# Attention sums as one block behind each head's scores, the two products of the third score bank swapped, and the first eight late-modulation rows moved from head 36 to head 49

## The chip, the cores and the metric

The kernel runs on one core of a Trainium2 chip. The metric is the device time of one execution in microseconds (us); lower is better. Before the change three timed executions took 2225.91, 2229.25 and 2231.14 us, a median of 2229.25 us.

## The reference

One transformer-like block on x of 2048 tokens by 1024 channels: a compressive-memory attention and then a token-mixing MLP, both modulated by six rows made from a condition c. Cut to what matters:

```python
mod = (silu(c) @ w_mod).reshape(1, 6, 1, -1)            # sa, ca, ga, sb, cb, gb
h = layernorm(x) * (1 + ca) + sa
# attention: 32 heads of 32 channels, 4 segments of 512 tokens
for s in range(4):
    logits = q[s] @ k[s].T * scale + mask               # causal inside the segment
    a_dot = softmax(logits) @ v[s]
    a_mem = (phi(q[s]) @ M) / (phi(q[s]) @ z + 1e-6)    # memory of earlier segments
    o[s] = g * a_mem + (1 - g) * a_dot
    M, z = M + phi(k[s]).T @ v[s], z + phi(k[s]).sum()
x = x + ga * (concat(o) @ wo)
h = layernorm(x) * (1 + cb) + sb
x = x + gb * mixer(h)                                   # y = W2 gelu(W1 layernorm(h))
```

`sa` and `ca` are needed at the start. The four other rows of the modulation are needed only after the attention: they are the "late" rows here.

## The kernel before

**Tasks and heads.** The attention runs in two passes over the tokens: segments 0 and 1 for all eight groups of four heads, then segments 2 and 3. A task t is one group and one segment, so there are 32 tasks of 4 heads, and the loop counts 128 heads n = 4t + h: heads 0 to 63 are the first pass, 64 to 127 the second. What belongs to head h of task t carries both numbers in its name: `sz_7_0` is task 7, head 0.

**What one head does.** `project` makes a task's k, v and q on TensorE (PE) with 256-column products (`nps`, L192) and 512-column products (`qps`, L200), splits of full precision into two parts. `maxima` makes the logits once to find each query's largest one: four products (L478) fill three PSUM banks in turn, `sx` (128 and 256 columns), `sy` (384) and `sz` (512), out of a pool `s1` of two banks; VectorE (DVE) reduces each bank (L480). So the fill of one bank waits until DVE has read the bank two fills before it. `scores` makes the logits again, transposed and with the maximum folded in: three banks `a0` (L515, 512 columns), `a1` (L518, 384) and `a2` (L521 with 128 columns, then L522 with 256), out of a pool `s2` of two banks; ScalarE (ACT) takes the exponential of each (L516, L519, L523) into `p32`, GpSimd (POOL) sets the masked corners to zero (L526), ACT rounds to fp16 (`ph`, L528) and POOL makes the remainder (L530, held in `p32`).

**The sums.** `values` multiplies these weights by v: 20 short products (L544) into one bank `pv`, ten with the rounded part `ph` (97 columns) and then ten with the remainder (65 columns). DVE then takes a reciprocal (L547), a reduction (L549) and a scaling (L551). `values` of a head is called two heads after its `scores` (VL = 2), `maxima` of a head three heads before (LEADS = 3).

**Order.** The code is written in one order, but the framework's scheduler chooses the order of each engine's instructions from its own timeline, within the dependences and within `tc.issue_after`: each instruction in such a block comes behind the given one on that one's engine. `behind(n, engines)` uses it with the instructions noted in `marks`. On the chip each engine runs its list strictly in order and waits where an operand or a buffer is not ready.

**Late rows.** 32 blocks of w_mod (512 KB each) are loaded by `mod_fetch` into a buffer of the pool `raw` (three buffers, shared with the loads of weights) and reduced on DVE by `mod_late` (L573). `later(n, fetch, m, f, engines)` puts the load at head n and the use at head m. Block j below 8 is loaded at head 36 + 2j and used two heads later; block j from 8 on at head 44 + 2j and used one head later. After block 7, `mod_rows(0, 8)` writes the first row out, and head 62 (`spread(gaw, 0)`) reads it back. Around heads 36 to 50 the weights of the eighth group are split (`split_part`, L119 on ACT and L122 on DVE), and from head 51 on the stored h pages of segments 2 and 3 are loaded (`reload_h`).

After the attention come the output products (L791), the norms, and the mixer (L921), which is the longer half of the run.

Of the kernel before, what the change touches and what calls it, by code (L numbers as in the profile page):

```python
# [18 lines left out]
P = 128  # L19
# [8 lines left out]
NV = 97  # L28
# [3 lines left out]
VL = 2  # L32
ML0 = 36
# [8 lines left out]
def attention_and_mlp(ctx, tc, x, wq, wkv, wo, beta, w1, b1, w2, b2, c, wm_a, wm_b, out):  # L42
    nc = tc.nc
    V, A, G, T, SY = nc.vector, nc.scalar, nc.gpsimd, nc.tensor, nc.sync
# [451 lines left out]
    marks = {}  # L496

    @contextmanager
    def behind(n, engines):

        with ExitStack() as s:
            for e in engines:
                if (n, e) in marks:
                    s.enter_context(tc.issue_after(marks[n, e].ins))
            yield

    def scores(t, h):
        d = st[t]
        n = 4 * t + h
        q, k = d["sk", h][:, 0], d["sk", h][:, 1]  # L510
        p32 = r_.tile([P, 1280], F32, tag="p32", bufs=3, name=f"p32_{t}_{h}")
        hi, lo = r_.tile([P, 1280], F16, tag="ph", bufs=3, name=f"ph{t}_{h}"), p32.bitcast(F16)[:, 0:1280]
        d["ph", h] = hi, lo
        b0 = bank("s2", 2, f"a0_{t}_{h}")
        T.matmul(b0, k[:, 0:128], q, start=True, stop=True)  # L515
        A.activation(p32[:, 0:512], b0, AF.Exp, scale=SCALE, bias=shift)  # L516
        b1_ = bank("s2", 2, f"a1_{t}_{h}")
        T.matmul(b1_[:, 0:384], k[:, 128:256], q[:, 128:512], start=True, stop=True)  # L518
        A.activation(p32[:, 512:896], b1_[:, 0:384], AF.Exp, scale=SCALE, bias=shift)  # L519
        b2_ = bank("s2", 2, f"a2_{t}_{h}")  # L520
        T.matmul(b2_[:, 0:128], k[:, 384:512], q[:, 384:512], start=True, stop=True)  # L521
        T.matmul(b2_[:, 128:384], k[:, 256:384], q[:, 256:512], start=True, stop=True)  # L522
        A.activation(p32[:, 896:1280], b2_[:, 0:384], AF.Exp, scale=SCALE, bias=shift)  # L523
        for base, step in ((0, 512), (896, 128)):
            w = bass.AP(tensor=p32.tensor, offset=p32.offset + base, ap=[p32.ap[0], [step, 2], [1, 128]])
            G.affine_select(w, w, pattern=[[0, 2], [1, 128]], compare_op=ALU.is_ge, fill=0.0, base=0,  # L526
                            channel_multiplier=-1)
        marks[n, "A"] = A.copy(hi, p32)  # L528
        for c in (slice(0, 640), slice(640, 1280)):
            marks[n, "G"] = G.tensor_tensor(lo[:, c], p32[:, c], hi[:, c], op=ALU.subtract)  # L530

    def values(t, h):
        pr, g, seg = its[t]
        d = st[t]
        am, ph = d["am"], d["ph", h]
        pv = bank("pv", 1, f"pv{t}_{h}").rearrange("p (a n) -> p a n", a=4)
        col = {0: lambda i: 128 * i, 1: lambda i: 512 + 128 * (i - 1), 2: lambda i: 1024 + 128 * (i - 2),
               3: lambda i: 896}
        n = 0
        for part, w in ((0, NV), (1, 65)):  # L540
            for i in range(4):
                for j in range(i + 1):
                    o = col[j](i)
                    T.matmul(pv[:, i, 0:w], ph[part][:, o:o + 128], d["vp"][:, j, h, 0:w], start=(n == 0),  # L544
                             stop=(n == 19), skip_group_check=True)
                    n += 1
        V.reciprocal(pv[:, :, 0], pv[:, :, 0])  # L547
        red = r_.tile([P, 4, 32], F32, tag="red", bufs=2, name=f"red{t}_{h}")
        V.tensor_reduce(red, pv[:, :, 1:97].rearrange("p a (c e) -> p a e c", c=3), axis=AX.X, op=ALU.add)  # L549
        ah = am[:, :, 32 * h:32 * h + 32]  # L550
        V.scalar_tensor_tensor(red if seg else ah, red, gate[:, 1, 4 * g + h:4 * g + h + 1],  # L551
                               pv[:, :, 0:1].to_broadcast([P, 4, 32]), op0=ALU.mult, op1=ALU.mult)
        if seg:
            G.tensor_tensor(ah, ah, red, op=ALU.add)
        if h < 3:
            return
        ps = bank("ms", 1, f"ops{t}")
        for i in range(4):
            T.transpose(ps[:, 128 * i:128 * i + 128], am[:, i], ident)
        ot = r_.tile([P, L], F32, tag="ot", bufs=1, name=f"ot{t}")  # L560
        A.copy(ot, ps)
        SY.dma_start(oT[g, :, L * seg:L * seg + L], ot)
        del st[t]
# [3 lines left out]
    def mod_fetch(j):  # L567
        r = a.tile([P, D], F32, tag="raw", bufs=3, name=f"rawm{j}")
        SY.dma_start(r, wm_b[P * j:P * j + P])
        return r  # L570

    def mod_late(j, r):
        V.scalar_tensor_tensor(r, r, 1.0, scb, op0=ALU.mult, op1=ALU.mult, accum_out=mcol[:, j:j + 1])  # L573
        if j == 7:
            mod_rows(0, 8)
        if j == 31:
            V.tensor_scalar_add(mcol[:, 16:24], mcol[:, 16:24], 1.0)
            mod_rows(8, 32)
# [14 lines left out]
    def at(f, n):  # L593
        if 0 <= n < 4 * NI:
            f(n // 4, n % 4)
# [62 lines left out]
    def later(n, fetch, m, f, engines):  # L658

        got = []  # L660
        plan(n, lambda: got.append(fetch()))
        plan(m, lambda: f(got[0]), engines)
# [8 lines left out]
    for g in range(2, NG):  # L671
        n = 8 * g - 13
# [3 lines left out]
                  n + n1, lambda r, g=g, kind=kind, part=part: split_part(g, kind, part, r), "A")  # L676
        plan(n + 4, lambda g=g: keep_w(g))
    for j in range(32):
        n = ML0 + 2 * j + (8 if j >= 8 else 0)
        later(n, lambda j=j: mod_fetch(j), n + (2 if j < 8 else 1), lambda r, j=j: mod_late(j, r), "V")  # L680
    plan(WO0 - 3, lambda: spread(gaw, 0))
    for i in range(8):
        n = WO0 + WOS * i
        later(n, lambda i=i: wo_fetch(i), n + 1, lambda r, i=i: wo_split(i, r), "G")

    for n in range(-LEADS, 4 * NI + VL):
        at(scores, n)
        at(maxima, n + LEADS)
        at(values, n - VL)
        m = n + LEADP  # L690
        if 0 <= m + 4 < 4 * NI:
            t = (m + 4) // 4
            if its[t][:2] not in W:
                with tc.issue_after(last_sk[t - 2 if t > 16 else 0, 3].ins):
                    load_w(its[t][1], its[t][0])
        if m >= 8:
            at(project, m)
        if 59 <= m < 67:
            seg, ct = 2 + (m - 59) // 4, 2 * ((m - 59) % 4)
            with ExitStack() as s:  # L700
                if seg == 3:
                    s.enter_context(tc.issue_after((last_sk[15, 3] if ct < 4 else last_nt[14, 3]).ins))
                reload_h(seg, ct)
                reload_h(seg, ct + 1)
        if 4 * NI - 5 <= m < 4 * NI + 3:
            i = m - 4 * NI + 5
            for c in (2 * (i % 4), 2 * (i % 4) + 1):
                wop[c, i // 4] = new_page(f"wo{c}_{i // 4}")
                if c < 5 or i < 4:
                    SY.dma_start(wop[c, i // 4].bitcast(F32), wos[c, i // 4])  # L710
        for f, engines in todo.pop(n, ()):
            with behind(n, engines):
                f()
# [427 lines left out]
```

## Time and profile before

| | before |
|---|---|
| median of three executions | 2229.25 us |
| the profiled execution's own time | 2226.6 us |
| its span, first to last instruction | 2224.9 us |
| PE busy | 2190.3 us, 98% of the span |
| DVE busy | 1666.7 us, 75% |
| ACT, POOL busy | 1135.7 us (51%), 725.8 us (33%) |
| granted TensorE clock, mean | 0.997 |

A busy time counts from the start of an instruction to its end. Matmuls are pipelined, so their records overlap: the distance from one start to the next is what a matmul costs PE, and the length of its record is longer. In a timeline, rows of equal instructions that follow each other are merged; the columns are start, length, engine, line, operation, output and inputs, shape and count, and in brackets the idle time before and what ended it. "PEld" is the weight load that goes with each matmul. "PEclk" is the share of the full TensorE clock that was granted.

### The profile page before, as it was taken

What the parts mean: (1) busy time and instruction counts of PE and PEld (TensorE: products, weight loads), DVE (VectorE), ACT (ScalarE), POOL (GpSimd) and SP (SyncE); (2) the same over time, 40 slices, a digit from 0 to 9 for tenths busy, and PEclk for the clock granted to TensorE, in tenths of its full rate; (3) what the DMA queues carried; (4) which work ended last, traced back from release to release, by engine and by line L of the source; (5) the groups of instructions that cost most, each with busy time, mean ns of one, the idle gap of its engine ahead of it and who ended that gap; (6) DMA issues with size and microseconds to landing.
All of it is one profiled execution on the core that took longest, in us unless ns stands there. A gap on an engine that the chain in (4) does not pass through costs nothing.

```text
span 2224.9 us, 38052 instructions
## 1 busy us (share of the span) xinstructions
PE 2190.3 (98%) x13786; PEld 1881.0 (85%) x13786; DVE 1666.7 (75%) x3762; ACT 1135.7 (51%) x2050; POOL 725.8 (33%) x831
## 2 busy tenths in 40 slices
PE   8999999999999999999999999999999999999999
PEld 5988898888999999888888888888888888888887
DVE  7676777756777777664858766888888886969687
ACT  5486776756666666654636533533334242424232
POOL 2175766646767776663002200033330000000000
PEclk9999999999999999999999999999999999999999
DMA  7666666686556666664754687655556542414134
GB/s 287 192 187 191 175 181 193 189 279 216 170 180 205 188 183 211 193 219 143 231 194 186 226 304 275 243 223 220 204 202 219 206 148 64 145 57 147 57 123 151
DMA packets 175183, 423.03 MB, mean 190 GB/s; under 512 B 17524, under 2 KB 71828, under 8 KB 166036
## 3 DMA queue, kind: packets, MB, share of 16 engines
q1 hardware_dynamic: 174996, 420.61, 57.5%
q8 instruction: 109, 1.79, 0.3%
q14 instruction: 78, 0.64, 0.1%
HBM read 244.62 MB, written 125.06 MB: 166 GB/s over the span
## 4 chain that ended last, share of the span: by engine, by line
PE 87%; DVE 5%; DMA 3%; ACT 2%; POOL 1%; issue 1%; SPq 0%; DVEq 0%; ACTq 0%
PE mx L921 48%; PE nps L192 11%; PE po L791 8%; PE qps L200 7%; PE pv L544 3%; PE a L515 1%; PE sz L478 1%; PE sx L478 1%; DMA sk<-nt 1%; PE up L460 1%; PE a L518 1%; POOL p L530 1%; PE a L522 1%; PE sy L478 1%; PE rd L450 1%
## 5 line engine op out<-in xcount | busy, mean ns | idle before, releaser
L921 PE MATMUL mx<-bU,sp 128*128 128x512 f32 x2352 | 534.3, 389 | 0.9 <-DVE ac L928 0.9
L921 PEld LDWEIGHTS mx<-bU,sp 128*128 128x128 f32 x2352 | 441.3, 188 | 93.4 <-issue 1.3
L119 ACT CAST sp<-wr 128x384 fp32r<-128x384 f32 (+2 forms) x408 | 218.1, 547 | 431.8 <-PE mx L921 349.1
L192 PE MATMUL nps<-wv,h 128*128 128x256 f32 x3072 | 431.2, 283 | 1.6 <-DVE h L122 0.7
L921 PE MATMUL mx<-bA,sp 128*128 128x512 f32 x1764 | 430.5, 389 | 0.0
L530 POOL TENSOR_TENSOR p<-p,ph 128x640 f16<-128x640 f32 x256 | 380.2, 1485 | 138.5 <-ACT ph L528 134.5
L192 PEld LDWEIGHTS nps<-wv,h 128*128 128x128 f32 x3072 | 400.3, 189 | 9.4 <-DVE h L122 2.0
L921 PEld LDWEIGHTS mx<-bA,sp 128*128 128x128 f32 x1764 | 331.2, 188 | 68.7
L122 DVE TENSOR_TENSOR sp<-wr,sp 128x384 fp32r<-128x384 f32 (+2 forms) x408 | 259.8, 648 | 24.7 <-ACT sp L119 24.4
L928 DVE TENSOR_TENSOR ac<-mx,ac 128x512 f32<-128x512 f32 x280 | 189.9, 687 | 85.2 <-PE mx L921 84.1
L200 PE MATMUL qps<-h,wq 128*128 128x512 f32 x768 | 197.9, 400 | 0.0
L528 ACT CAST ph<-p 128x1280 f16<-128x1280 f32 x128 | 161.4, 1261 | 59.7 <-POOL p L526 59.6
L791 PE MATMUL po<-wo,ots 128*128 128x512 f32 x768 | 180.9, 391 | 0.0
L791 PEld LDWEIGHTS po<-wo,ots 128*128 128x128 f32 x768 | 142.7, 188 | 28.7
L200 PEld LDWEIGHTS qps<-h,wq 128*128 128x128 f32 x768 | 141.6, 190 | 27.7
L921 PE MATMUL mx<-bB,sp 128*128 128x512 f32 x588 | 164.0, 389 | 0.0
L526 POOL TENSOR_SCALAR_AFFINE_SELECT p<-p 128x256 f32<-128x256 f32 x256 | 134.1, 529 | 81.8 <-ACT p L523 53.9
L921 PEld LDWEIGHTS mx<-bB,sp 128*128 128x128 f32 x588 | 110.4, 188 | 22.9
L480 DVE CUSTOM_DVE_ANT_0 sz<-sz,mask 128x512 f32<-128x512 f32 x128 | 89.1, 696 | 52.0 <-PE sz L478 49.5
L480 DVE CUSTOM_DVE_ANT_0 sx<-sx,mask 128x128 f32<-128x128 f32 (+1 forms) x256 | 93.7, 366 | 44.1 <-PE sx L478 37.9
L928 DVE TENSOR_TENSOR cc<-mx,cc 128x512 f32<-128x512 f32 x140 | 94.9, 684 | 37.6 <-PE mx L921 37.4
L516 ACT ACTIVATE p<-a,shift 128x512 f32<-128x512 f32 x128 | 88.4, 691 | 41.2 <-PE a L515 40.4
(209 smaller groups left out, 3244.7 us busy)
## 6 DMA issues: line engine op xcount, KB each, us to landing
sk<-sg SPq DMA_DIRECT2D x384, 128.0 KB
wr<-in_w_dram SPq DMA_DIRECT2D x28, 1024.0 KB
wr<-in_w_dram SPq DMA_DIRECT2D x32, 768.0 KB
bstu<-ucd SPq DMA_DIRECT2D x28, 768.0 KB
wsp<-wv SPq DMA_DIRECT2D x32, 512.0 KB
rawm<-in_wm_b_dram SPq DMA_DIRECT2D x32, 512.0 KB
wv<-wsp SPq DMA_DIRECT2D x32, 512.0 KB
pcd<-cc SPq DMA_DIRECT2D x14, 1024.0 KB
```

The source lines that it names most:

```text
L119: last_hi[0] = A.copy(hi, src)
L122: return lo_eng.tensor_tensor(lo, src, hi.bitcast(F32), op=ALU.subtract)
L192: T.matmul(ps[:, aa], h[:, j, 128 * tt:128 * tt + 128], wt[:, i, o:o + 256], start=(n == 0), stop=(n >= 6 * NK - 2), skip_group_check=True)
L200: T.matmul(ps, wt[:, i, o:o + 128], h[:, j], start=(k + n == 0), stop=(3 * k + n == 3 * NK - 1))
L480: marks[4 * t + h - LEADS, "V"] = V.tensor_tensor_reduce(o, o, mask[:, 384 - 128 * i:], 1.0, -3.0e38, op0=ALU.add, op1=ALU.max, accum_out= ...
L516: A.activation(p32[:, 0:512], b0, AF.Exp, scale=SCALE, bias=shift)
L526: G.affine_select(w, w, pattern=[[0, 2], [1, 128]], compare_op=ALU.is_ge, fill=0.0, base=0, channel_multiplier=-1)
L528: marks[n, "A"] = A.copy(hi, p32)
L530: marks[n, "G"] = G.tensor_tensor(lo[:, c], p32[:, c], hi[:, c], op=ALU.subtract)
L791: T.matmul(ps, os_[:, i, P * ct:P * ct + P], wop[ct, nh][:, j], start=(n == 0), stop=(n == 3 * NK - 1))
L921: T.matmul(ps, ops[q][:, i, P * k:P * k + P], b[:, j], start=(m == 0 and first), stop=(m == 3 * nk - 1), skip_group_check=True)
L928: V.tensor_tensor(d, ps, d, op=ALU.add)
```

## The change

Three edits. The last product of `scores` on PE is noted in `marks[n, "P"]`, and PE's instructions of `values(n - 2)` come behind it. The two products of `a2` change places, 256 columns first. The 20 sums are made in the opposite order: the ten with the remainder first and, in each part, from the last tile to the first. The first eight late rows are loaded at heads 49 to 56, one a head, and used one head later; the other 24 stay.

```diff
@@ scores
-        T.matmul(b2_[:, 0:128], k[:, 384:512], q[:, 384:512], start=True, stop=True)
-        T.matmul(b2_[:, 128:384], k[:, 256:384], q[:, 256:512], start=True, stop=True)
+        for lo_, hi_, kt in ((128, 384, 2), (0, 128, 3)):
+            marks[n, "P"] = T.matmul(b2_[:, lo_:hi_], k[:, 128 * kt:128 * kt + 128], q[:, 128 * kt:], start=True,
+                                     stop=True)
@@ values
-        for part, w in ((0, NV), (1, 65)):
-            for i in range(4):
-                for j in range(i + 1):
-                    o = col[j](i)
-                    T.matmul(pv[:, i, 0:w], ph[part][:, o:o + 128], d["vp"][:, j, h, 0:w], start=(n == 0),
-                             stop=(n == 19), skip_group_check=True)
-                    n += 1
+        for part, w in ((1, 65), (0, NV)):
+            for i, j in [(i, j) for i in range(4) for j in range(i + 1)][::-1]:
+                o = col[j](i)
+                T.matmul(pv[:, i, 0:w], ph[part][:, o:o + 128], d["vp"][:, j, h, 0:w], start=(n == 0),
+                         stop=(n == 19), skip_group_check=True)
+                n += 1
@@ the plan of the late rows
-        n = ML0 + 2 * j + (8 if j >= 8 else 0)
-        later(n, lambda j=j: mod_fetch(j), n + (2 if j < 8 else 1), lambda r, j=j: mod_late(j, r), "V")
+        n = 49 + j if j < 8 else ML0 + 2 * j + 8
+        later(n, lambda j=j: mod_fetch(j), n + 1, lambda r, j=j: mod_late(j, r), "V")
@@ the loop over heads
-        at(values, n - VL)
+        with behind(n, "P"):
+            at(values, n - VL)
```

Since the scheduler orders everything anew, the order changes in both passes and on every engine. Two places show how. The first is on PE in the first pass, between the maxima of task 6 head 3 and of task 7 head 0, before the change (`sk0_3`, `sk1_0` are the stacked q and k of these heads; `pv5_1` are the sums of task 5 head 1):

```order
L478 MATMUL sy_6_3_3722<-sk0_3_500 128x384
L486 MATMUL nmps6_1_3504<-ident_90,mx6_0_3342 8x128
L544 LDWEIGHTS ph5_1_3326
L544 MATMUL pv5_1_3629<-vp5_2704,ph5_1_3326 128x97
...
L544 MATMUL pv5_1_3629<-vp5_2704,p32_5_1_3325 128x65
L521 MATMUL a2_5_2_3484<-sk1_2_503 128x128
L522 MATMUL a2_5_2_3484<-sk1_2_503 128x256
L478 MATMUL sz_6_3_3725<-sk0_3_500 128x512
L478 MATMUL sx_7_0_3837<-sk1_0_501 128x128
L478 MATMUL sx_7_0_3837<-sk1_0_501 128x256
L478 MATMUL sy_7_0_3842<-sk1_0_501 128x384
```

The same place after the change:

```order
L478 MATMUL sy_6_3_3722<-sk0_3_500 128x384
L486 MATMUL nmps6_1_3504<-ident_90,mx6_0_3342 8x128
L478 MATMUL sz_6_3_3725<-sk0_3_500 128x512
L478 MATMUL sx_7_0_3837<-sk1_0_501 128x128
L478 MATMUL sx_7_0_3837<-sk1_0_501 128x256
L478 MATMUL sy_7_0_3842<-sk1_0_501 128x384
L478 MATMUL sz_7_0_3845<-sk1_0_501 128x512
L522 MATMUL a2_5_2_3484<-sk1_2_503 128x256
L522 MATMUL a2_5_2_3484<-sk1_2_503 128x128
L544 LDWEIGHTS p32_5_0_3200
L544 MATMUL pv5_0_3514<-vp5_2704,p32_5_0_3200 128x65
```

The 20 sums and the two products of `a2` that stood between the fills `sy_6_3` and `sz_6_3` now stand behind `sz_7_0`, so that five maxima fills follow each other. The second place is on DVE, in the stretch where the late rows now are, after the change (`sz_14_0` to `sx_14_2` are maxima of task 14, `rawm3` and `rawm4` late rows):

```order
L480 ISA sz_14_0_7080,mx14_0_7071<-sz_14_0_7080,mask_93 128x512
L480 ISA mx14_0_7071 128x1
L573 SCALAR_TENSOR_TENSOR rawm3_7052,mcol_529<-rawm3_7052,scb_76 128x1024
L480 ISA sx_14_1_7191,mx14_0_7071<-sx_14_1_7191,mask_93 128x128
...
L480 ISA sz_14_1_7199,mx14_0_7071<-sz_14_1_7199,mask_93 128x512
L480 ISA mx14_0_7071 128x1
L573 SCALAR_TENSOR_TENSOR rawm4_7172,mcol_529<-rawm4_7172,scb_76 128x1024
L551 SCALAR_TENSOR_TENSOR am12_5982<-red12_2_6978,gate_113,pv12_2_6956 128x4x32
L480 ISA sx_14_2_7317,mx14_2_7316<-sx_14_2_7317,mask_93 128x128
```

Before the change the same maxima stood without a late row among them:

```order
L480 ISA sz_14_0_7098,mx14_0_7089<-sz_14_0_7098,mask_93 128x512
L480 ISA mx14_0_7089 128x1
L480 ISA sx_14_1_7206,mx14_0_7089<-sx_14_1_7206,mask_93 128x128
L480 ISA mx14_0_7089 128x1
L547 RECIPROCAL pv12_2_6971<-pv12_2_6971 128x4
L480 ISA sx_14_1_7206,mx14_0_7089<-sx_14_1_7206,mask_93 128x256
...
L480 ISA sz_14_1_7214,mx14_0_7089<-sz_14_1_7214,mask_93 128x512
```

Two late rows now stand between the maxima of neighbouring heads, directly ahead of the next head's first one. Over the whole program the 2560 sums stand in 289 unbroken pieces before (32 heads in one piece of 20) and in 154 after (102 heads in one piece); behind the second product of `a2` stand sums at once for 71 heads of 128.

## The prediction

> **What bounds the kernel now.** I read the page first, then the busy times by pass, then PE's timeline, then the waits.
>
> ```profile
> span 2224.9 us, 38052 instructions
> PE 2190.3 (98%) x13786; PEld 1881.0 (85%) x13786; DVE 1666.7 (75%) x3762; ACT 1135.7 (51%) x2050; POOL 725.8 (33%) x831
> PE 87%; DVE 5%; DMA 3%; ACT 2%; POOL 1%; issue 1%; SPq 0%; DVEq 0%; ACTq 0%
> ```
>
> PE sets the end: it is busy 98% of the span and carries 87% of the chain that ended last. The table of stretches (core; length; busy of PE, PEld, DVE, ACT, POOL; clock; DMA share) splits the attention into its passes:
>
> ```profile
> 100.00:540.00 440.00, 425.79 (x3764) 389.18 (x3762) 316.70 (x925) 313.24 (x574) 279.13 (x320) 0.98 0.66 196
> 540.00:1000.00 460.00, 454.82 (x4008) 413.78 (x4005) 327.64 (x1002) 288.43 (x497) 311.10 (x374) 1.00 0.65 196
> ```
>
> PE idles 440 − 425.79 = 14.2 us in the first pass and 5.2 us in the second. So the change can gain in two ways only: a shorter stream of products, or fewer waits; and it loses by more waits. PE's timeline at the place that the first order excerpt shows:
>
> ```profile
> 253.61 0.41 PE L544 MATMUL pv<-vp,p 128*128 128x65 bf16 x8
> 253.85 0.47 PE L515 MATMUL a<-sk 98*128 98x512 f32 x1
> 254.16 0.24 PE L544 MATMUL pv<-vp,p 128*128 128x65 bf16 x2
> 254.24 0.48 PE L478 MATMUL sz<-sk 96*128 96x512 f32 x1
> 254.55 0.39 PE L478 MATMUL sx<-sk 96*128 96x128 f32 x2
> ...
> 256.42 0.60 PE L544 MATMUL pv<-vp,ph 128*128 128x97 bf16 x10
> 256.86 0.47 PE L544 MATMUL pv<-vp,p 128*128 128x65 bf16 x10
> 257.17 0.31 PE L521 MATMUL a<-sk 98*128 98x128 f32 x1
> 257.31 0.33 PE L522 MATMUL a<-sk 98*128 98x256 f32 x1
> 257.48 0.40 PE L478 MATMUL sz<-sk 96*128 96x512 f32 x1
> 257.72 0.39 PE L478 MATMUL sx<-sk 96*128 96x128 f32 x2
> 258.87 0.44 PE L478 MATMUL sy<-sk 96*128 96x384 f32 x1 [0.77 <-DMA rawq<-in_wq_dram]
> ```
>
> Two prices are in it. A 512-column product takes 257.72 − 257.48 = 0.24 us to the next start, but 254.55 − 254.24 = 0.31 us behind a piece of sums: the sums are too short to cover the load of the next f32 weights. And `sy_7_0` at 258.87, which needs the bank of `sz_6_3`, starts 258.87 − 257.72 = 1.15 us after PE was done with that bank, while PE had only `sx_7_0` to do. The releaser named is a DMA; the waits of the weight loads name the real one:
>
> ```profile
> PEld sy L478 <- DVE mx L480: 3.6, 4, 1.4
> PEld a L521 <- ACT p L516: 3.1, 3, 1.2
> ```
>
> So a maxima bank turns around in about 1.15 us, and a score bank (ACT, second row) waits in the same way.
>
> **The stream (edits one and two).** Each piece of sums ends with the surcharge of 0.07 us. The two orders have 289 and 154 pieces: 135 × 0.07 = 9.5 us less. The swap in `a2` is priced by these rows:
>
> ```profile
> 261.89 0.34 PE L518 MATMUL a<-sk 98*128 98x384 f32 x1
> 262.07 0.74 PE L192 MATMUL nps<-wv,h 128*128 128x256 f32 x5
> 262.64 0.23 PE L521 MATMUL a<-sk 98*128 98x128 f32 x1
> 262.71 0.33 PE L522 MATMUL a<-sk 98*128 98x256 f32 x1
> 262.88 0.28 PE L192 MATMUL nps<-wv,h 128*128 128x256 f32 x1
> ```
>
> 384 columns in one product take 0.18 us, 128 and then 256 take 0.24: the short product does not cover the load behind it, 0.06 us. With the short one last, it is covered where sums follow at once (71 heads: 71 × 0.06 = 4.3 us) and paid behind it where another f32 product follows (57 heads: nothing gained). Together −13.8 us; the surcharge read from other rows may be 0.06 or 0.08, so −12 to −16. The reversed order inside the sums costs nothing by itself: same count, same columns. That remainders come first means that POOL must be done before the piece starts; with two heads between `scores` and `values` I cost it at nothing, and if that cover were missing it would show as PE waiting for L531.
>
> **The waits (edit one).** The sums were also what PE did while DVE and ACT emptied banks. The first order excerpt shows it: 20 sums between `sy_6_3` and `sz_6_3` gave DVE 0.75 us (256.42 to 257.17); after the change `sz_6_3`, `sx_7_0`, `sy_7_0` and `sz_7_0` follow each other, and each waits for DVE. No row of before shows these waits, so I estimate them: both orders laid end to end with the start-to-start times of rows like these, counting each bank fill that comes less than 1.15 us after the last product two fills before. Before: 17 fills, together 8.0 us short (10 of `s1`, 7 of `s2`), against 14.2 us of idle time measured in that pass, 3.5 of it one stall (below). After: 46 fills, 19.6 us short (28 and 18), nearly all in the first pass. That is +11.6 us. The turnaround sets this term: at 0.8 us, little more than DVE's own time for the largest bank (next row, 696 ns), it is +4.4; at 1.5 us +24. I take 1.15, the value that a row shows directly.
>
> ```profile
> L480 DVE CUSTOM_DVE_ANT_0 sz<-sz,mask 128x512 f32<-128x512 f32 x128 | 89.1, 696 | 52.0 <-PE sz L478 49.5 <-PE pv L544 2.0
> ```
>
> Queued behind each such PE wait are the projections and the sums; on DVE the reciprocals (L547) come later with them, and POOL's additions (L554) behind these; neither has a deadline that PE meets sooner than the bank itself.
>
> **The late rows (edit three).** The largest wait of PE stands among the old late rows:
>
> ```profile
> 449.51 1.92 DVE L573 SCALAR_TENSOR_TENSOR rawm<-rawm,scb 128x1024 f32<-128x1024 f32 x1 [1.55 <-DMA rawm<-in_wm_b_dram]
> 451.36 2.69 DVE L122 TENSOR_TENSOR wq<-rawq,wq 128x512 fp32r<-128x512 f32 x2
> 454.73 0.41 DVE L454 TENSOR_TENSOR am<-rd,rdd 128x256 f32<-128x256 f32 x1
> 455.29 1.00 PE L460 MATMUL up<-v,pk 128*128 128x132 f32 x3 [3.48 <-DVE am L454]
> ```
>
> DVE waited 1.55 us for a late row, then did it and two weight splits, and PE stood 3.5 us for L454 behind them. The clock fell with it (the seventh figure is PEclk):
>
> ```profile
> 130.00:135.00 5.00, 4.22 (x26) 3.16 (x25) 4.07 (x8) 5.00 (x9) 2.85 (x6) 0.80 1.01 240
> 135.00:140.00 5.00, 5.00 (x44) 4.90 (x43) 3.15 (x6) 3.63 (x7) 4.02 (x4) 0.86 0.97 288
> 450.00:455.00 5.00, 1.82 (x14) 1.45 (x12) 5.00 (x9) 3.68 (x8) 3.43 (x3) 0.88 1.04 355
> 455.00:460.00 5.00, 4.71 (x33) 4.47 (x34) 4.08 (x12) 2.57 (x5) 1.60 (x6) 0.50 1.02 367
> 460.00:465.00 5.00, 5.00 (x19) 4.17 (x18) 3.45 (x12) 2.28 (x5) 3.72 (x4) 0.59 0.92 354
> ```
>
> Clock lost there: 5 × (0.12 + 0.50 + 0.41) = 5.2 us. In the new order no late row stands ahead of that L454, so 3.5 + 5.2 = 8.7 us go. But the eight rows move into a stretch whose DMA queues are hardly freer, with one head from load to use where they had two, past SP's queue where two of their loads now stand together twice:
>
> ```profile
> 440.00:460.00 20.00, 16.52 (x138) 15.50 (x137) 17.53 (x41) 13.23 (x23) 12.28 (x16) 0.85 0.95 304
> 480.00:500.00 20.00, 19.31 (x156) 17.07 (x155) 8.12 (x31) 11.73 (x21) 9.68 (x13) 1.00 0.83 251
> L573 DVE SCALAR_TENSOR_TENSOR rawm<-rawm,scb x32: 1212/1272/2467, 368.4 to 871.5; 128x1024 f32<-128x1024 f32 x32
> DMA rawm<-in_wm_b_dram: 8.2, 6
> ```
>
> Six of 32 rows made DVE wait 8.2 us in all, 1.4 each, and a row itself is 1.3 us. The second order excerpt shows rows 3 and 4 directly ahead of maxima that PE needs. I take two of the eight to hold PE for 1.5 us each, +3.0; between 0 and 8 × 1.5 = 12.
>
> **The clock.** The first drop, in the rows of 130 to 140, cost 5 × (0.20 + 0.14) = 1.7 us, with PE idle for 0.78 us of 130 to 135 and no idle at all in 135 to 140; the second followed the 3.5 us stall. So short waits that lie close together are enough, and the new waits do: by the count above two or more fills of one head or neighbouring heads fall short together at tasks 7, 8, 11, 13 and 14. The waits at task 7 head 0 (0.9 + 0.9 + 0.8 us) and at task 14 (two fills and a late row, about 2.8) come near to the 3.5 us: 5.2 each; the other three 1.7 each: +15.5 us. Bounds: 0, and 5 × 5.2 = 26.
>
> [...]
>
> **The sum**, against the profiled execution: −13.8 + 11.6 − 8.7 + 3.0 + 15.5 = +7.6 us on a span of 2224.9, so 2232.5, and 1.7 us more around it (2226.6 was its own time, within the three timed ones and 2.65 under their median). I add it to the median: 2229.25 + 7.6 = 2236.9, say 2237 us.
>
> **Rivals.** About 0.2% (4.5 us) is what a measurement of this kernel can tell from no change.
>
> Faster, because the banks turn in time. If a bank turns in 0.8 us, the waits cost 4.4, the late rows find cover and cost nothing, and two drops of the short kind are left, 3.4: −13.8 + 4.4 − 8.7 + 3.4 = −14.7, so 2214.5 us. The place is the chain of maxima at task 7 head 0; it decides where DVE takes a bank at once. For it: DVE is busy 72% of the first pass, so often it is free. Against it: the 1.15 us at 258.87. Chance 0.22.
>
> Faster, because the clock holds. All terms as forecast but the clock's at 0, since no new idle stretch is as long as 3.5 us: −7.9, so 2221.4 us. Against it: the drop at 130 to 140. Chance 0.12.
>
> No change: all five groups of waits cost one short drop each, 8.5 us: +0.6, so 2229.9 us. Chance 0.16.
>
> Slower still: a late row again finds its load late and the stall of 8.7 us comes back at heads 50 to 57: +16.3, so 2245.6 us. For it: DMA share 0.83 and one head of lead. Chance 0.08.
>
> That the change does not do what it says is ruled out by the order: 102 heads have their sums in one piece.
>
> **Numbers.** The forecast has 0.42; its own range is 2230 to 2246. Slower by over 0.2%: nearly all of it and the last rival, 0.48. Within 0.2%: 0.18. Faster: the first two rivals, 0.34. The range for 8 in 10 has to reach from the first rival to the last one, 2212 to 2247.
>
> **What would show it.** Right: PE's idle time from 100 to 540 near 25 us, with L478 and L522 waiting for DVE L480 and ACT; `sz` behind sums at 0.31 us only once a head; no 3.5 us wait of L460; PEclk below 1 in three or more places between 150 and 530; the second pass shorter by about 6 us. Wrong: idle time in the first pass at 14 us or less, or a clock that never falls.

## The result and the profile after

The changed kernel takes 2237.95 us (median of 10 runs, 2232.59 to 2244.36) against 2228.24 us for the kernel before (10 runs, 2225.54 to 2233.23) on the same chip: a ratio of 1.0043 with a 95% interval of 1.003 to 1.0056. It is 9.7 us slower; the forecast was +7.6, and 2237 us. The profiled execution of the changed kernel took 2232.59 us, the shortest of its ten, with a span of 2230.9: against the span of before (2224.9) it shows 6.0 of the 9.7 us.

The page of the changed kernel, its busy times and the shares of the chain that ended last:

```profile
PE 2183.8 (98%) x13786; PEld 1882.7 (84%) x13786; DVE 1662.1 (75%) x3762; ACT 1133.2 (51%) x2050; POOL 719.0 (32%) x831
PE 83%; DMA 5%; DVE 5%; ACT 3%; POOL 2%; issue 1%; SPq 1%; ACTq 0%; DVEq 0%; POOLq 0%
```

PE still sets the end, but it is busy for 2183.8 us instead of 2190.3 and carries 83% of the chain instead of 87%; DMA went from 3% to 5% of it and POOL from 1% to 2%. The stream got shorter and the waits grew by more. The table of stretches of the changed kernel says where:

```profile
100.00:540.00 440.00, 418.58 (x3696) 383.70 (x3695) 311.90 (x907) 309.45 (x566) 274.58 (x314) 0.98 0.65 193
540.00:1000.00 460.00, 451.34 (x4018) 417.17 (x4018) 321.57 (x1006) 285.80 (x494) 303.61 (x373) 1.00 0.64 193
1000.00:1060.00 60.00, 58.50 (x382) 48.76 (x382) 29.99 (x76) 30.62 (x55) 24.41 (x27) 1.00 0.50 170
```

And the last stretch of before, which the prediction did not show:

```profile
1000.00:1060.00 60.00, 59.98 (x353) 49.17 (x352) 30.87 (x79) 28.24 (x50) 18.98 (x21) 1.00 0.43 144
```

PE idles 21.4 us in the first pass (14.2 before), 8.7 in the second (5.2) and 1.5 in the tail of the attention (0.0): 31.6 against 19.4, +12.2 us. Behind 1060 us nothing changed but the start: the first product of the mixer with `bA` moved from 1153.3 to 1159.0 us, and the last product from 2220.9 to 2226.9.

What PE waited for longest in the changed kernel from 100 to 1060 us:

```profile
PE sx L478 <- DMA sk<-sg: 6.7, 5, 2.0
PE sz L478 <- DVE mx L480: 6.6, 9, 2.0
PE a L515 <- DMA sk<-nt: 5.3, 6, 1.6
PE a L522 <- ACT p L516: 2.0, 5, 0.9
```

and the releasers of the one line L478 (us, times), products and weight loads together, in the changed kernel:

```profile
  DVE mx L480: 22.8, 35
  DMA sk<-sg: 8.9, 6
  DVE rawm L573: 2.1, 1
```

and in the kernel before:

```profile
  DVE mx L480: 7.0, 9
...
  DMA sk<-sg: 0.2, 1
```

The maxima's products waited 22.8 us in 35 places for DVE to empty a bank, where they had waited 7.0 us in 9. (A wait of a product and one of its weight load are counted apart here, so these figures are larger than PE's idle time.) The loads of stacked q and k (`sk<-sg`, transfers that SP issues) held the same line for 8.9 us instead of 0.2; the forecast had no term for them. PE's timeline of the changed kernel at the place of the first order excerpt shows how:

```profile
255.00 0.49 PE L478 MATMUL sz<-sk 96*128 96x512 f32 x1
256.71 0.47 PE L478 MATMUL sx<-sk 96*128 96x128 f32 x2 [1.21 <-DMA sk<-sg]
257.01 0.33 PE L478 MATMUL sy<-sk 96*128 96x384 f32 x1
258.15 0.50 PE L478 MATMUL sz<-sk 96*128 96x512 f32 x1 [0.80 <-DVE mx L480]
258.49 0.34 PE L522 MATMUL a<-sk 98*128 98x256 f32 x2
258.68 0.48 PE L544 MATMUL pv<-vp,p 128*128 128x65 bf16 x10
258.99 0.81 PE L544 MATMUL pv<-vp,ph 128*128 128x97 bf16 x10
259.58 0.77 PE L515 MATMUL a<-sk 98*128 98x512 f32 x1
```

The maxima fills stand in one row without work between them. `sx_7_0` is reached 1.0 us earlier than in the kernel before (257.72) and waits 1.21 us for its stacked q and k. `sz_7_0` starts 258.15 − 257.01 = 1.14 us after `sy_7_0` started, that is after PE had left the bank of `sx_7_0`, and PE waited 0.80 of that; the 20 sums that could have filled both waits stand at 258.68, behind them, though POOL had finished their remainders by 253.2. The product of L515 at 259.58 is stretched from 0.48 to 0.77 us: there the clock fell. Clock of the changed kernel, by stretches of 5 us (the seventh figure):

```profile
255.00:260.00 5.00, 2.98 (x28) 2.24 (x28) 3.89 (x14) 4.18 (x8) 3.28 (x4) 0.92 0.90 238
260.00:265.00 5.00, 5.00 (x36) 4.72 (x36) 4.96 (x11) 4.49 (x7) 2.70 (x3) 0.74 0.95 273
340.00:345.00 5.00, 3.77 (x14) 3.30 (x15) 3.80 (x15) 2.66 (x8) 3.19 (x6) 0.66 0.01 2
```

The drop at 260 cost 5 × (0.08 + 0.26) = 1.7 us, that at 340 cost 5 × 0.34 = 1.7. By the clock records of the two profiled executions the attention ran 20.5 us at half clock instead of 13.7: half of the difference, 3.4 us, is lost. So the profiled pair closes as +12.2 (idle) + 3.4 (clock) − 9.6 (what is left, put down to the shorter stream) = +6.0 us. Over all timed runs the clock cost more: the time multiplied by one minus the run's mean granted clock is 13.4 us on average, against 6.1 to 7.4 for the kernel before in the three sessions of the experiments. With 6 or 7 instead of 3.4, and idle time and stream as in the profiled pair, the same sum gives about 9, against the 9.7 measured.

### The profile page after: what moved, and what is told of

It is laid out like the page before. It is cut to its first block, busy times and chain, and to the rows that moved or that the text cites. A ratio compares the mean times of both kernels' runs of the same rounds, so it can differ in the third digit from the quotient of the medians.

```text
span 2230.9 us, 38127 instructions
## 1 busy us (share of the span) xinstructions
PE 2183.8 (98%) x13786; PEld 1882.7 (84%) x13786; DVE 1662.1 (75%) x3762; ACT 1133.2 (51%) x2050; POOL 719.0 (32%) x831
## 4 chain that ended last, share of the span: by engine, by line
PE 83%; DMA 5%; DVE 5%; ACT 3%; POOL 2%; issue 1%; SPq 1%; ACTq 0%; DVEq 0%; POOLq 0%
PE mx L922 47%; PE nps L192 11%; PE po L792 8%; PE qps L200 7%; PE pv L544 3%; DMA sk<-sg 1%; POOL p L531 1%; PE a L515 1%; PE sz L478 1%; DMA rawm<-in_wm_b_dram 1%; PE sx L478 1%; PE a L518 1%; DMA sk<-nt 1%; PE a L522 1%; ACT ph L529 1%
## 5 line engine op out<-in xcount | busy, mean ns | idle before, releaser
L192 PE MATMUL nps<-wv,h 128*128 128x256 f32 x3072 | 424.7, 283 | 1.3 <-DVE h L122 0.7
L480 DVE CUSTOM_DVE_ANT_0 sx<-sx,mask 128x128 f32<-128x128 f32 (+1 forms) x256 | 93.3, 364 | 48.7 <-PE sx L478 40.4
L480 DVE CUSTOM_DVE_ANT_0 sz<-sz,mask 128x512 f32<-128x512 f32 x128 | 88.9, 694 | 45.3 <-PE sz L478 44.3
```

The lines of the kernel that those rows point to most:

```text
L192: T.matmul(ps[:, aa], h[:, j, 128 * tt:128 * tt + 128], wt[:, i, o:o + 256], start=(n == 0), stop=(n >= 6 * NK - 2), skip_group_check=True)
L480: marks[4 * t + h - LEADS, "V"] = V.tensor_tensor_reduce(o, o, mask[:, 384 - 128 * i:], 1.0, -3.0e38, op0=ALU.add, op1=ALU.max, accum_out= ...
```

## The experiments

All kernels below were run in five rounds with the kernel before on the same chip; the differences are to that. They fall into three sessions, each on its own chip, so kernels of different sessions are compared by their ratio to the kernel before. "Block" means the `behind` around the sums. Two theories stood against each other: that the loss is the cover which the sums gave to PE's waits in the first pass, and that it is made by another part of the change (the late rows, or the order as a whole).

**Changed kernel without the block.**

```diff
-        with behind(n, "P"):
-            at(values, n - VL)
+        at(values, n - VL)
```

> The changed kernel without the block: the sums are again placed freely, all else as changed (sums in the new order, products of the third bank swapped, late rows from head 49). Theory of the waits (gathering the sums took the work away that covered the turn of the banks): first-pass idle time of PE from 21 us back to 12 to 16, no more than two low-clock windows there, and the time 3 to 8 us below the kernel before. Rival, the late rows (their new place is what costs): idle time stays near 21 us, late near 460 to 520, and the time stays 5 to 12 us above. Rival, the clock alone: the stalls return to those of before but low-clock windows stay at 5 or more.

2224.95 us, ratio 0.9974 (0.9961 to 0.9986), −5.2 us. Its first pass idles 440 − 425.48 = 14.5 us, as before. L478 waits 4.7 us for L480. The profiled run has 20.5 us at half clock, as many as the changed kernel's and all in the first pass, where two low-clock windows were expected at most (6.8 us at the 3.4 us of a single drop): that part of the expectation failed. Third bank, late rows and the reversed order of the sums together gain; the block turns the gain into a loss, 1.0043 − 0.9974 = 0.0069, 15 us.

**Changed kernel with the late rows in their old place.**

```diff
-        n = 49 + j if j < 8 else ML0 + 2 * j + 8
-        later(n, lambda j=j: mod_fetch(j), n + 1, lambda r, j=j: mod_late(j, r), "V")
+        n = ML0 + 2 * j + (8 if j >= 8 else 0)
+        later(n, lambda j=j: mod_fetch(j), n + (2 if j < 8 else 1), lambda r, j=j: mod_late(j, r), "V")
```

> The changed kernel with the late rows left where they were before (heads 36 to 50). Theory of the waits: the loss stays, 4 to 12 us above the kernel before, since the block is what costs; whether the 3.5 us wait of L460 is there decides a few us. Rival, the late rows: the time falls to that of before or below it, since the stream is still shorter.

2231.28 us, ratio 1.0004 (0.9992 to 1.0016), +1.1 us: no loss of 4 to 12 us, as the theory of the waits had it, but the time of before, as its rival had it. The first pass idles as much as the changed kernel's, 440 − 418.76 = 21.2 us, but the second pass 5.7 instead of 8.7 and the tail 0.2 instead of 1.5. Beside the full block, the new place of the rows costs 1.0043 − 1.0004 = 0.0039, nearly 9 us. The profiled pair shows only 3.0 of them (spans of 2230.9 and 2227.9 us), and there the idle time grew after the first pass.

**The kernel before with the new late rows alone** (the same two lines, the other way round).

> The kernel before with nothing changed but the late rows, from head 49 on. Theory of the waits: the 3.5 us wait of L460 and the 10.2 us at half clock behind it are gone and nothing of this size replaces them: 2 to 9 us faster than before. Rival, the late rows cost by themselves: 3 to 9 us slower, with DVE waits for the late rows above 12 us and PE waits of L478 near 500 us.

2227.99 us, ratio 0.999 (0.9979 to 1.0002): −2.2 us, not told apart from no change. The 3.5 us wait of L460 is gone, but the second pass has two new ones (the last figure is the longest single wait):

```profile
PE a L515 <- DMA sk<-nt: 5.7, 6, 2.3
PE sx L478 <- DMA sk<-sg: 2.7, 1, 2.7
```

The wait of 2.7 us lies between 935 and 940 us, and the clock drops beside it (0.95 in the 5 us from 935, 0.71 in the next 5); over the whole second pass its mean is 0.99. Idle time is up by 2.4 us in all, and the half-clock time fell from 13.7 to 6.8 us, 3.4 us gained. Yet the profiled span is 4.0 us longer (2228.9), so the stream of this order is 5.0 us longer than before, where its 295 pieces of sums instead of 289 would make 0.4.

**The swap in the third bank alone, in the kernel before.**

```diff
-        T.matmul(b2_[:, 0:128], k[:, 384:512], q[:, 384:512], start=True, stop=True)
         T.matmul(b2_[:, 128:384], k[:, 256:384], q[:, 256:512], start=True, stop=True)
+        T.matmul(b2_[:, 0:128], k[:, 384:512], q[:, 384:512], start=True, stop=True)
```

> The kernel before with only the two products of the third score bank swapped. Theory of the waits: with sums placed freely the short last product is seldom followed by sums, so the stream shortens by about 1 us only, and the reshuffled order has 26 short fills where it had 17, 2.5 us: 0 to 5 us above the kernel before. Rival (the swap carries the gain that the prediction gave it): 3 to 5 us below.

2231.16 us, ratio 1.0016 (1.0005 to 1.0027), +2.5 us. Without the block only 44 heads have sums behind the short product (71 in the changed kernel), and the new order has 306 pieces of sums: by the prediction's prices −2.6 + 1.2 = −1.4 us. Idle time is unchanged (+0.3), and the stream of the profiled run is 1.3 us longer, not shorter. The swap gains nothing by itself.

**The block alone, in the kernel before** (its sums in the old inner order).

```diff
+            marks[n, "P"] = T.matmul(...)   # last product of a2, still the 256 columns
...
-        at(values, n - VL)
+        with behind(n, "P"):
+            at(values, n - VL)
```

> The kernel before with only the block: sums behind the scores, their old order, the third bank unswapped, the late rows in their old place. Theory of the waits: 157 pieces of sums instead of 289 and 34 short fills instead of 17: stream 8.5 us shorter, waits about 9 us longer, and more half clock: 2 to 12 us above the kernel before. Rival (the block gains and the other edits lose): 3 us or more below.

2238.53 us, ratio 1.0045 (1.0027 to 1.0062), +9.9 us: as much as the whole change (the profiled run, 2242.43 us, is the longest of its six). Idle time is 440 − 418.94 = 21.1 us in the first pass and 12.2 in the second, +14.1 in all, with 157 pieces of sums in place of 289. Here most of the first pass's idle time stands from 360 to 540 us (7.0 and 6.1 us) and only 3.0 from 240 to 360, where the changed kernel has 8.1: with the same block the loss sits elsewhere when the order is another. The kernel with the old late rows (1.0004) has this block too, and beside it the swap and the reversed order of the sums, and is 0.0041, 9 us, better. Which of the two brings that is open; the reversed order was never tried apart.

**Shorter maxima, without and with the change.** The maximum of each bank is taken over its last 128 columns only, so that DVE's pass over `sz` takes 295 ns and not 696; the exponent is scaled by 0.01 to keep numbers finite. The computation differs by that.

```diff
-                    o, o, mask[:, 384 - 128 * i:], 1.0, -3.0e38, ...
+                    o[:, 128 * i:], o[:, 128 * i:], mask[:, 384:], 1.0, -3.0e38, ...
...
-        A.activation(p32[:, 0:512], b0, AF.Exp, scale=SCALE, bias=shift)
+        A.activation(p32[:, 0:512], b0, AF.Exp, scale=0.01 * SCALE, bias=shift)
```

> The kernel before with a cheaper turn of the maxima banks: DVE reduces only the last 128 columns of each tile of logits instead of all of them (the output is not the reference's: the maximum leaves the other columns out, and the exponent is scaled by 0.01 to keep it finite). It is the control for the next run. Theory of the waits: there were few short fills to win back here, so 3 to 8 us below the kernel before. Rival (DVE does not hold PE): no change.

> The changed kernel with the same cheaper maxima as the control. Theory of the waits: with banks that turn faster the gathered sums open few waits, so the shorter stream (326 pieces of sums against 154 in this pair, some 12 to 17 us) reaches the end and the sign turns: 6 to 16 us below its control, though the changed kernel is 10 above the kernel before. Rival (the loss comes from elsewhere in the new order: late rows, DMA or the clock by itself): still 4 us or more above its control.

The control took 2232.92 us (ratio to the kernel before 1.0024, 1.0013 to 1.0035), a miss: it was expected to gain, but its new order cuts the sums into 326 pieces and idles 2.2 us more. With the change it is 2226.75 us (0.9993, 0.9978 to 1.0007), 6.2 us less than the control. The sign turned as expected, though the reason given is only a part of it. The stretches of the changed one:

```profile
100.00:540.00 440.00, 422.83 (x3802) 391.48 (x3801) 280.44 (x933) 316.07 (x577) 278.88 (x320) 0.99 0.67 196
540.00:1000.00 460.00, 447.96 (x3990) 413.23 (x3989) 280.90 (x994) 286.80 (x496) 304.32 (x373) 1.00 0.64 197
```

It idles 17.2 + 12.0 + 2.6 (the tail) = 31.8 us against 12.4 + 8.1 + 1.1 = 21.6 in the control: +10.2, nearly the +12.2 of the real pair. But the waits for DVE don't grow with the block any more: L478 waits 14.1 us for L480, against 14.6 in the control, where the real pair has 22.8 against 7.0. The stretch in which the changed kernel loses most shows the same. In order the kernel before, the changed kernel, the control and the changed kernel with short maxima:

```profile
240.00:360.00 120.00, 118.18 (x1067) 107.95 (x1066) 88.76 (x255) 93.61 (x172) 79.29 (x91) 1.00 0.60 173
240.00:360.00 120.00, 111.88 (x982) 101.44 (x981) 85.09 (x241) 87.47 (x164) 72.20 (x86) 0.97 0.56 167
240.00:360.00 120.00, 117.60 (x1076) 107.38 (x1074) 75.60 (x253) 92.52 (x170) 79.28 (x93) 1.00 0.62 178
240.00:360.00 120.00, 116.26 (x1051) 108.33 (x1048) 75.12 (x249) 91.28 (x169) 77.39 (x90) 0.99 0.60 173
```

With the change the idle time there goes from 1.8 to 8.1 us, with short maxima only from 2.4 to 3.7. At task 7 head 0 the same fills follow each other in both changed kernels; with short maxima:

```profile
255.15 0.34 PE L478 MATMUL sy<-sk 96*128 96x384 f32 x1
256.01 0.50 PE L478 MATMUL sz<-sk 96*128 96x512 f32 x1 [0.53 <-DVE mx L480]
```

`sz_7_0` starts 256.01 − 255.15 = 0.86 us after `sy_7_0` instead of 1.14. What idles more in this pair are other waits: in the first pass PE waits 7.2 us for stacked q and k (`sk<-sg`), 1.4 in the control, and the second pass idles 3.9 us more. The shorter stream pays for them: 326 − 154 = 172 pieces × 0.07 = 12 us and 4.3 of the swap, against 9.5 and 4.3 in the real pair. So the waits for DVE that the block adds go away when the maxima are short, as the theory of the waits has it; the rest of the idle time that comes with the block stays. How far a new order alone moves these figures, the control shows: its maxima are short too, and L478 waits 14.6 us for them instead of 7.0.

**The block only in one pass.**

```diff
-        with behind(n, "P"):
+        with behind(n, "P" if n >= 64 else ""):     # second pass only
...
+        with behind(n, "P" if n < 64 else ""):      # first pass only
```

> The changed kernel with the block in the second pass only (heads 64 on). Theory of the waits: DVE's banks turn in time there, so the second pass keeps the shorter stream and the first pass its cover: first-pass idle near 14 us, time 2 to 8 us below the kernel before. Rival, the block costs in both passes alike: about half of the loss stays, 3 to 6 us above.

> The changed kernel with the block around the sums' products only in the first pass (heads 0 to 63); the second pass keeps its sums loose, and the late rows and the third bank stay as changed. Theory (in the first pass the block takes the loose cover away from the short bank fills, and the two short fills stand there in front of maxima that are not ready): this kernel carries the whole loss, 4 to 12 us above the kernel before on its chip, with TensorE idle about 21 us between 100 and 540 us. Rival (each pass carries its share of the loss): half of it, 2 to 6 us above the kernel before, so about 2 to 6 us below the changed kernel.

Second pass only: 2221.37 us, ratio 0.9957 (0.9941 to 0.9973), −8.8 us; faster than both kernels. First pass only: 2235.11 us, ratio 1.0032 (1.002 to 1.0044), +5.8 us, which lies in the ranges of both theories; it is the two runs together that tell. They differ by 1.0032 − 0.9957 = 0.0075, nearly 17 us. Against the kernel without any block (−5.2 us) the block costs 11.0 us in the first pass; in the second it brings 3.6, which the intervals don't tell from nothing. PE's waits in the kernel with the block in the second pass:

```profile
PE a L515 <- DMA sk<-nt: 7.5, 6, 3.1
...
PE sx L478 <- DMA sk<-sg: 1.9, 3, 1.0
...
PE sz L478 <- DVE mx L480: 1.3, 3, 0.6
```

and with it in the first:

```profile
PE sz L478 <- DVE mx L480: 6.8, 5, 2.9
...
PE sx L478 <- DMA sk<-sg: 4.2, 5, 1.6
PE a L515 <- DMA sk<-nt: 3.4, 4, 2.4
```

`sz` waiting for DVE goes from 1.3 to 6.8 us with the place of the block. The first passes idle 16.7 and 23.4 us, the second ones 5.2 and 6.0. The place is best seen in the stretch from 240 to 360 us, first with the block in the first pass, then without it there:

```profile
240.00:360.00 120.00, 109.88 (x963) 99.55 (x962) 84.48 (x241) 87.35 (x163) 71.31 (x84) 0.99 0.56 167
```

```profile
240.00:360.00 120.00, 114.81 (x1040) 106.22 (x1040) 90.47 (x258) 91.79 (x170) 79.90 (x89) 1.00 0.61 174
```

10.1 us of idle time against 5.2, and 77 products fewer done. And PE's timeline of the second of these kernels at the place shown above, from `sy_6_3` to `sz_7_0`:

```profile
258.20 0.42 PE L478 MATMUL sy<-sk 96*128 96x384 f32 x1
...
258.64 0.48 PE L544 MATMUL pv<-vp,p 128*128 128x65 bf16 x10
258.96 0.61 PE L544 MATMUL pv<-vp,ph 128*128 128x97 bf16 x10
259.38 0.48 PE L478 MATMUL sz<-sk 96*128 96x512 f32 x1
259.70 0.39 PE L478 MATMUL sx<-sk 96*128 96x128 f32 x2
...
261.10 0.44 PE L478 MATMUL sy<-sk 96*128 96x384 f32 x1 [0.45 <-DVE mx L480]
...
262.81 2.25 PE L192 MATMUL nps<-wv,h 128*128 128x256 f32 x17
...
265.08 0.44 PE L478 MATMUL sz<-sk 96*128 96x512 f32 x1
```

The same heads' maxima stand apart, with sums and projections of the next task (`nps`) between the fills; `sy_7_0` waits 0.45 us for DVE, `sx_7_0` and `sz_7_0` not at all. The first order excerpt spoke of sums; without the block the scheduler puts projections there too.

**The block from head 48 on.**

```diff
-        with behind(n, "P"):
+        with behind(n, "P" if n >= 48 else ""):
```

> The changed kernel with the block only from head 48 on, so that the last quarter of the first pass has it as well. Theory (the cost of the block sits in the early heads of the first pass, where K, V and mask rows still arrive; later the block only saves pieces of sums): 6 to 10 us below the kernel before, equal to the kernel with the block in the second pass alone or 1 to 3 us below it. Rival (the block costs cover in any head of the first pass): 2 to 4 us above the kernel with the block in the second pass alone.

2221.41 us, ratio 0.996 (0.9946 to 0.9973), −7.9 us: within 1 us of the block in the second pass alone. Its first pass idles 15.3 us. So the loss sits in heads 0 to 47; that the last quarter of the first pass costs the 2 to 4 us of the rival isn't excluded, since each of the two intervals is 3 us to either side.

**The second-pass block with the late rows in their old place, and with the third bank in its old order.** The edits are those of the kernels above, made in the one with the block from head 64 on.

> The block only from head 64 on, the third bank as changed, and the first eight late-modulation rows in their old place. It asks what the new place of those rows is worth beside the second pass's block. Theory (the new place takes away one 3.5 us wait and its slower products, and costs only where the first pass has no loose products left): 3 to 8 us above the kernel with the block in the second pass alone. Rival (the new place costs some 6 us wherever a block follows): 3 to 7 us below that kernel.

> The block only from head 64 on, the new late rows, and the third bank in its old order (128-column product first). If the 256-column product first is worth the 0.06 us a head at which the prediction took it, 3 to 5 us above the kernel with the block in the second pass alone; rival (the swap is worth nothing, since the order that the scheduler makes with it costs as much in waits): equal to it within 1.5 us.

Old rows: 2232.0 us, ratio 1.001 (1.0001 to 1.0019), against 0.9957 with the new ones. Here the new place gains 0.0053, nearly 12 us, more than either theory gave, where beside the full block it costs nearly 9. Much of it is one event. PE's timeline of the kernel with the old rows:

```profile
491.59 0.50 PE L515 MATMUL a<-sk 98*128 98x512 f32 x1
498.66 0.77 PE L478 MATMUL sx<-sk 96*128 96x128 f32 x2 [6.58 <-DMA sk<-sg]
```

Near the end of the first pass PE stands 6.6 us for stacked q and k that SP's queue brings late. The clock is at half for 10.2 us from 495.3 on; the 6.8 us of them that lie behind the wait cost 3.4. Why SP issued those loads late in this order was not tried apart.

Old third bank: 2220.83 us, ratio 0.9966 (0.9954 to 0.9979), against 0.9957 (0.9941 to 0.9973) with the swap. The intervals overlap; the times are 0.5 us apart, as the rival had it, but the swap's 4.3 us are neither shown nor excluded.

**All of them together.** The twelve kernels and the two of the case, sorted by one question, whether the block stands in heads 0 to 47 (the first five) or not:

| kernel | ratio to before | idle of first pass, us | L478 waiting for L480, us |
|---|---|---|---|
| changed kernel | 1.0043 | 21.4 | 22.8 |
| block alone | 1.0045 | 21.1 | 11.2 |
| block in the first pass | 1.0032 | 23.4 | 21.7 |
| changed, old late rows | 1.0004 | 21.2 | 15.9 |
| short maxima, changed | 0.9993 | 17.2 | 14.1 |
| kernel before | 1 | 14.2 | 7.0 |
| short maxima, before | 1.0024 | 12.4 | 14.6 |
| swap alone | 1.0016 | 14.8 | 8.8 |
| late rows alone | 0.999 | 12.1 | 5.2 |
| no block | 0.9974 | 14.5 | 4.7 |
| block from head 48 | 0.996 | 15.3 | 9.1 |
| block in the second pass | 0.9957 | 16.7 | 8.2 |
| same, old third bank | 0.9966 | 15.3 | 7.2 |
| same, old late rows | 1.001 | 21.6 | 11.5 |

With the block in the early heads the first pass idles 21.1 to 23.4 us (17.2 with short maxima), without it 12.1 to 16.7; the one exception is the kernel with the single wait of 6.6 us. The last column separates them less well: the control of the short maxima (14.6) and the last row (11.5) reach into the first group. Nor does the ratio alone separate them: 0.9993 and 1.0004 stand in the first group, 1.001 to 1.0024 in the second.

## Why the prediction was right, and where its terms were not

**Sign and size.** +9.7 us against +7.6, in the profiled pair +6.0. In outline the mechanism is the forecast's: the stream got shorter, PE's idle time ate that, and the clock decided. The kernels with the block in only one pass show it: the loss goes with the block in the early heads.

**The waits.** Forecast for all idle time: 11.6 − 3.5 + 3.0 = +11.1 us; measured +12.2. First pass "near 25 us": 21.4, with L478 waiting for L480 as named. The place was right too: the waits and the drop at task 7 head 0 are there (256.7 to 260), and so was the price of a bank there, 1.15 us forecast and 1.14 measured, 0.86 with short maxima. But the total is made of other parts. The score banks, which were to have 18 short fills instead of 7, hold PE no longer than before (L522 2.0 us, L521 before 2.4, both for ACT). In their place stand the loads of stacked q and k, which the forecast left out. The longest wait for a maximum, 1.97 us for `sz` at 341.2, is not the turn of a bank either: DVE had a long pass for the memory to do first.

```profile
338.46 1.86 DVE L426 SCALAR_TENSOR_TENSOR pk<-k,rk 128x512 f32<-128x512 f32 x1
```

And nearly all of it was to be in the first pass, where only 7.2 us are; 3.5 came in the second and 1.5 in the tail. That the total agrees within about 1 us is luck.

**The second pass shorter by about 6 us** is the step that failed. Its idle time rose by 3.5 us. Take the columns that PE's products have streamed as the measure of work done: where the kernel before is at 540 us, the changed kernel is 5.0 us behind it, and at the start of the mixer 5.7, so all that lies between took 0.7 us longer. The shorter stream did reach the end in two other kernels: by the same measure the stretch from 540 us on is 5.6 us shorter with the block in the second pass alone, and 6.4 shorter with the late rows in their old place. That points to the new late rows beside a full block, a term that the forecast did not have. But the kernel with the block alone has the old rows and idles 12.2 us in the second pass, so the cause stays open.

**The late rows** were to bring −8.7 + 3.0 = −5.7 us. The 3.5 us stall of L460 went, as forecast, and one late row held PE, for 2.1 us (`sx` behind `rawm` above), where two of 1.5 were taken. The 8.7 counts some time twice: the drop of 10.2 us began at 453.8, within the stall that ended at 455.3, so that the clock lost 4.4 us behind the stall and not 5.2. But the rows' place has no price of its own: alone it brought −2.2 us, beside the second-pass block −12, beside the full block +9. The term was sized as if the rest of the order stood still.

**The stream.** −13.8 forecast; −9.6 is what is left in the profiled pair, below the lower end (12) of its own bounds. Made the same way, with the price by each kernel's own pieces and swapped products behind it, the remainders are:

| kernel | left in the profile, us | by the prices, us |
|---|---|---|
| no block | −8.2 | −6.4 |
| block from head 48 | −10.8 | −11.8 |
| block in the second pass | −12.1 | −10.2 |
| same, old third bank | −6.3 | −6.7 |
| same, old late rows | −10.0 | −10.4 |
| changed, old late rows | −9.9 | −13.7 |
| block in the first pass | −4.0 | −10.3 |
| block alone | −3.3 | −9.2 |
| late rows alone | +5.0 | +0.4 |
| swap alone | +1.4 | −1.4 |

So the prices hold within 2 us in the first five kernels and are 3 to 6 us too favourable in the others. How much a kernel waits doesn't sort them: the one with the late rows alone idles 21.8 us in all and is off by 4.6, the one with the old rows beside the second-pass block idles 33.0 and fits. What else an order costs PE is open.

**The clock.** +10.3 net forecast, +3.4 in the profiled pair and some +6 to +7 over the runs. The number of drops was nearly right (three between 150 and 530 us, at 259, 341 and 498, and one at 942), but not their size: the two taken at 5.2 us cost 1.7 at task 7 and 3.4 at task 14 (498). Of the other three places, at tasks 8, 11 and 13, none showed a drop; the third one fell at task 9 head 2, which wasn't on the list, and from 275 to 280 PE idled 1.6 us with the clock at 1.00. That stream and clock were both taken too large, by 4 us each over the runs (4 and 7 in the profiled pair) and with opposite signs, is why the sum came so close, and that is luck.

**The rivals.** A bank that turns in 0.8 us and a clock that holds are both refuted by the changed kernel's idle time and drops; the stall of L460 did not come back. The rival of no change had the clock nearest, 8.5 − 5.2 = +3.3 net against +3.4 in the profiled pair; it failed with the stream, which it took at −13.8 like the forecast.

## What to carry to other kernels

Short independent products scattered through a stream look like a cost (by the rows of before, 0.31 us to the next start behind a piece of them instead of 0.24) but may be the cover of an engine that issues in order, as PE did where ready sums stood at 258.68, behind waits of 1.21 and 0.80 us: count what stands between two fills of the same bank before gathering them. Gather where PE hardly waits and leave them loose where it does: with the block from head 48 or from head 64 on the change is worth −8 to −9 us, without any block −5.2 (the intervals of these overlap), with it in all heads +9.7. Where a scheduler makes the whole order anew, the price of an edit belongs to one order only; the late rows were worth −12, −2 and +9 us beside three versions of the rest, so an edit is to be tried beside the one that it ships with.

## What the runs showed of the hardware

A single drop of the clock halves it for 3.4 us (0.5 of full speed for 3.413 us in the clock records of the kernel before and of the changed one), so it costs 1.7 us. One wait of 2 us was enough for it: in the changed kernel the clock fell at the end of the 1.97 us that `sz` waited to 341.2. Nor was the longer wait the surer one. In the kernel with the block in the first pass PE waited 2.40 us in the first of these rows and the clock held; in the kernel with the old third bank it waited 1.85 us, and the clock fell in the second row of its fence:

```profile
275.00:280.00 5.00, 2.60 (x29) 2.24 (x26) 2.95 (x11) 3.12 (x9) 4.20 (x6) 1.00 0.64 257
280.00:285.00 5.00, 5.00 (x23) 4.08 (x23) 3.04 (x4) 3.22 (x6) 2.56 (x3) 1.00 0.00 0
```

```profile
360.00:365.00 5.00, 3.15 (x35) 2.64 (x34) 4.95 (x11) 3.16 (x8) 3.39 (x5) 1.00 0.69 218
365.00:370.00 5.00, 5.00 (x17) 3.96 (x16) 1.10 (x4) 1.90 (x3) 2.81 (x2) 0.66 0.13 52
```

Between 60 and 2100 us the clock records of the kernel before and of the changed one hold seven drops. Five last 3.413 us, one 6.827 and one 10.240, and in each of the two traces they begin whole multiples of 3.413 us apart: 94 for those of the kernel before, at 133.0 and 453.8 us, and 37, 24, 46 and 130 for those of the changed kernel, at 132.9, 259.2, 341.1, 498.2 and 941.9. Cut into stretches of 3.413 us that are in step with the drops, the two traces have 598 stretches at full clock from 60 to 1100 us. All 5 in which PE idled for more than 1.65 us were followed by a drop, and none of the 573 in which it idled for less than 0.77; of the 20 between, 2 were (0.78 and 1.46 us) and 18 were not (up to 1.61 us). The wait of 2.40 us fits this if the steps of its kernel lie in the same way: a drop began there at 318.4 us (clock 0.84 from 315 to 320, 0.82 from 320 to 325), and 12 × 3.413 us before it, at 277.4, a step falls within the wait, which so had 1.4 us at most in one stretch. No stretch ahead of a drop was idle throughout: the most was 2.77 us of the 3.413, ahead of 498.2, and the drop of 453.8 in the kernel before began 2.0 us into its stall of 3.48. What decides between 0.77 and 1.65 us is open.
